# A recurrent-memory attention kernel: the forward loop's pools stay open, their tiles are reused by view in the backward loop, Wq is turned twice as often, and the crossbar loads are spread

## The chip, the core and the metric

The kernel runs on one core of one Trainium2 chip. Its time is the device time of one execution in microseconds (us); the time before is the median of three runs. One execution more was taken with the profiler. It gives for each instruction the engine, start, duration, and what it waited for. The engines are PE (matrix multiply; PEld are its weight loads), DVE (vector), ACT (scalar), POOL, and SP, which here only issues DMAs. ACT and POOL issue DMAs too.

## The reference

The reference is the forward pass and all gradients of a block with two branches. Branch B is a gated MLP. Branch A, which the change touches, is attention in 64 segments of 32 tokens, where eight memory rows pass from each segment to the next:

```
mem = mem0
for s in range(n_seg):                      # 64 segments
    h = concat([mem, xn[:, 32*s:32*s+32]])  # 8 + 32 rows, Dm = 640
    q, k, v = h @ Wq, h @ Wk, h @ Wv        # 32 heads of 128
    p = softmax(mask(q @ k.T * scale))
    o = (p @ v) @ Wo
    mem = o[:, :8]
    outs.append(o[:, 8:])
out = x + A(layernorm(x)) * silu(B(layernorm(x)))
grads = vjp(grad_out)                       # for x, mem0, Wq, Wk, Wv, Wo, w1, w3, w2
```

Only the eight memory rows are a chain from segment to segment, forward in the loop and backward in the gradient. The token rows can be computed at any time, and the kernel uses them to fill the gaps of the chain.

## The kernel before

The program runs in phases: layer norm and branch B forward, the first part of A, the forward recurrence (`recurrence`, L547), the backward recurrence (`phase4_Abwd`, L1073), then the weight gradients and B backward. The change lies in the two recurrences and between them.

**Forward recurrence.** `chain(t, gap)` (L591) does the memory rows of segment t; at named places (W0, W1, V0, W2, G1 to G6) it calls `gap`, which puts in token work of a block of three segments (`FILL`, L909). When the 64 steps are done, 13 units of token work (a block of 120 rows and four heads) are left. They are done in the tail (L1040), interleaved with a second stream, `work1` (L980), of which `fill(n)` takes n pieces. `work1` consists of:

- the first `out_proj` (L495), for the token rows 1344 to 1983. It takes 40 items: `ld` loads rows of 512 columns from the DRAM tensor OR (L509; a block that spans two stores takes two DMAs), `turn` transposes them on PE and copies them to oTm (L519, L520), `mm` multiplies by Wo (L526). Each item is two half items, with a yield after each. After eight items the sums are copied to `s_tok` (half on DVE, half on ACT) and stored to SR (L543). Six row buffers `orow` exist: four are quarters of the tile vt, two are tiles with the tag "kr" (L971, L972). Loads run five items ahead;
- beside every second half item, one turn of Wq (`wq_turn`, L717: five PE transposes of one head into bank bC and one copy to WqT, three in four on ACT, else on DVE);
- 16 gx blocks (`gx_block`, L1063: five matmuls of 512 columns, a copy, and after every second block a store to GX0);
- a second `out_proj` for the last 64 token rows, eight items.

The transposed weights WoT and WkT come through the crossbar: `turned_load` (L268), a transposing DMA issued by SP, 16 pieces each of 256x640 bf16 values. `w_ld(n)` (L712) issues n of those queued in `wfetch`. Of WoT, four go in gaps G2 and G4 of the last step and one in each step of the tail (L1050). WkT takes the place of Wq (tag "w2"), so it is allocated when Wq has been turned (L1002). Its pieces go with every second half item after that, with the gx blocks (L1014) and at the end (L1019).

**Backward recurrence.** `phase4_Abwd` opens pools of its own (L1094 to L1097) and makes its tiles (L1100 to L1110): four sets of row buffers (gors, gqvs, gPrs), and krb, which in the prologue serves as two more sets; vTb, which first holds gx blocks; gOTs, gdSs and others. Then come memsets on DVE (L1113), and banks in PSUM. The prologue (L1447 to L1474) does 19 units of token work: `ld`, `turn`, `dprob`, `dsoft`, `gmem`. It is interleaved with 32 further gx blocks (`gx_work`, L1432) and with 16 loads of WvT (L1464), which takes the place of Wo (tag "w3"). Then `chain` (L1171) goes from segment 63 to 0.

**What sets the order.** Each phase ends in `in_order(k, start)` (L273): it makes every instruction added since `start` follow the one written before it on its engine. An instruction written outside such a stretch, and two phases against each other, are ordered by the framework's scheduler, which takes what it finds ready; the wait for a buffer or a result is set by the framework too. When a pool is closed and another is opened over its addresses, the new pool's tiles wait for the readers and writers of the old pool as a whole. Inside one tile, reads and writes of different parts don't wait for each other.

Of the kernel before, what the change touches and what calls it, by code (L numbers as in the profile page):

```python
# [16 lines left out]
P = 128  # L17
# [371 lines left out]
def phase3_Afwd(k, W0, W4, Wv, Wk_):  # L389
# [4 lines left out]
    with tc.tile_pool(name="ast", bufs=1) as st:  # L394
# [5 lines left out]
        xPs = [st.tile([120, 4, P], BF16, name=f"xP{i}") for i in range(3)]  # L400
        PTs = [st.tile([120, 4, P], BF16, name=f"xPT{i}") for i in range(2)]
        oTm = st.tile([P, H, 32], BF16, name="oTm")
        first_part(k, Wv, Wk_, Wq, Wo, kTs, vt, hxs, qTs + xPs + PTs + [oTm])
        return recurrence(k, W0, W4, Wv, Wk_, Wq, Wo, kTs, vt, hxs, qTs, xPs, PTs, oTm)
# [90 lines left out]
def out_proj(k, Wo, x0, x1, acc, bank, orow, oTs, stok, q, done):  # L495
# [33 lines left out]
    for i in range(5):  # L529
        ld(i)  # L530
    yield
    turn(0)
    for i, (x, w, qd) in enumerate(items):
        ld(i + 5)
        turn(i + 1)
        mm(i, 0, 2)
        yield
        mm(i, 2, 4)
        if qd == 7:
            t = stok()  # L540
            for h in range(2):
                k.copy(t[0:w, 320 * h:320 * h + 320], acc[h][0:w, 0:320], eng='vs'[h])
            q.dma_start(k.SR[x:x + w, :], t[0:w, :])  # L543
        yield


def recurrence(k, W0, W4, Wv, Wk_, Wq, Wo, kTs, vt, hxs, qTs, xPs, PTs, oTm):  # L547
    nc, tc = k.nc, k.tc
    D, DC, S, H, HD, T = k.D, k.DC, k.S, k.H, k.HD, k.T
    with tc.tile_pool(name="achain", bufs=1) as ch, \  # L550
            tc.tile_pool(name="afill", bufs=1) as fl, \
            tc.tile_pool(name="aps", bufs=1, space=bass.MemoryType.PSUM) as ps, \
            tc.tile_pool(name="apm", bufs=1, space=bass.MemoryType.PSUM) as psm:
        bA, bB, bC = [psm.tile([P, 512], F32, name=f"bank{i}") for i in range(3)]
# [162 lines left out]
        def wq_turn(h):  # L717
            pt = bview(bC, P, DC, P, bf=True)
# [171 lines left out]
        def gap_of(t):  # L890
# [5 lines left out]
            def gap(g):  # L896
                FILL(g, t, at, kbatch)
                if t == T - 1:
                    if g == "G1":
                        w_alloc("o")  # L900
                        ld("q", *tail[0])
                        ld("q", *tail[1])
                    if g in ("G2", "G4"):
                        w_ld(2)
# [60 lines left out]
        batch = {t: b for t, b in batch.items() if t < T}  # L965
        for t in range(T):
            chain(t, gap_of(t))
        qm(T - 1)

        bA, bB, bC = [b_[:] for b_ in (bA, bB, bC)]  # L970
        orow = [vt[:, 512 * i:512 * i + 512] for i in range(4)]  # L971
        orow += [fl.tile([P, 512], BF16, name="orow", tag="kr", bufs=2)[:] for _ in range(2)]  # L972
        oTs = [oTm[:].rearrange("p a b -> p (a b)")[:, 512 * i:512 * i + 512].rearrange("p (a b) -> p a b", b=P) for i in range(2)]
        stok = lambda: ch.tile([P, D], BF16, name="s_tok", tag="oride")
        obank = lambda w: ps.tile([P, 4, w], BF16, name="opt", tag="x", bufs=5)
        done = {(k.NTL - 2, qd) for qd in SPL[0]}
        op = lambda x0, x1: out_proj(k, Wo, x0, x1, (bA, bB), obank, orow, oTs, stok, nc.gpsimd, done)
        X0, X1 = k.GB0, k.GB0 + 5 * P

        def work1():  # L980
            w_alloc("q")
            o = op(X0, X1)
            next(o)
            yield
# [7 lines left out]
            for _ in o:  # L992
                if n % 2 == 0 and n < 2 * H:
                    wq_turn(n // 2)
                n += 1
                yield
                if n == 40:
                    g_ld(0)
                if n == 2 * H:
                    while wfetch:  # L1000
                        w_ld(1)
                    w_alloc("k")  # L1002
                elif n > 2 * H and n % 2 == 0:
                    w_ld(1)
            g_ld(1)
            o = op(X1, S)
            next(o)
            for i, (x0, w) in enumerate(k.GXB[0:2]):
                for cg in range(4):
                    sg = ch.tile([P, 1024], BF16, name="g0st", tag="stg", bufs=2)  # L1010
                    for b in range(2):
                        gx_block(k, g0[i], sg, (bA, bB)[b], WT["o"], x0, w, cg, b, nc.scalar)
                        if b == 0:
                            w_ld(1)  # L1014
                        yield
            for _ in o:
                yield
            while wfetch:
                w_ld(1)  # L1019
# [4 lines left out]
        work = work1()  # L1024
# [15 lines left out]
        for i in range(len(tail) + 2):  # L1040
# [8 lines left out]
            if not WT.get("k"):  # L1049
                w_ld(1)  # L1050
# [22 lines left out]
def phase4_Abwd(k, out2, W4, WT):  # L1073
# [20 lines left out]
    with tc.tile_pool(name="gst", bufs=1) as st, tc.tile_pool(name="gchain", bufs=1) as ch, \  # L1094
            tc.tile_pool(name="gfill", bufs=1) as fl, \
            tc.tile_pool(name="gps", bufs=1, space=bass.MemoryType.PSUM) as ps, \
            tc.tile_pool(name="gpm", bufs=1, space=bass.MemoryType.PSUM) as psm:  # L1097
        NG = 4

        gors = [st.tile([120, 512], BF16, name=f"gor{i}") for i in range(NG)]  # L1100
        gqvs = [st.tile([120, 2, 512], BF16, name=f"gqv{i}") for i in range(NG)]
        vTb = st.tile([P, H, 40], BF16, name="vTt")
        bdm = st.tile([P, 16, 8], BF16, name="bdm")
        goxs = [st.tile([P, DC, 32], BF16, name=f"gox{i}") for i in range(2)]
        b16 = st.tile([P, 16], F32, name="b16")
        xpb = st.tile([P, 8, 2, 32], F32, name="xp")
        gdSs = [st.tile([120, 4, P], BF16, name=f"gdS{i}") for i in range(2)]
        gOTs = [st.tile([P, 4, P], BF16, name=f"gOT{i}") for i in range(2)]
        gPrs = [st.tile([120, 4, P], BF16, name=f"gPr{i}") for i in range(NG)]
        krb = st.tile([120, 2, 2048], BF16, name="krb")  # L1110
        bdf = goxs[0][:, 0:4, :].rearrange("p a b -> p (a b)").rearrange("p (a b) -> p a b", b=8)
        for tt in gOTs + gors + gdSs:
            nc.vector.memset(tt[:], 0.0)  # L1113
        bA, bB, bC = [psm.tile([P, 512], F32, name=f"gbank{i}") for i in range(3)]
# [19 lines left out]
        def loads(t):  # L1134
# [6 lines left out]
            Qst = ch.tile([P, 2, P], BF16, name="Qst", tag="Qst", bufs=2)  # L1141
# [4 lines left out]
        def load_k(t):  # L1146
            kr = krb[0:104, t % 2, :]
# [23 lines left out]
        def chain(t, gap):  # L1171
# [5 lines left out]
            bdP = ch.tile([P, 2, 16, 8], BF16, name="bdP", tag="bdP")  # L1177
# [54 lines left out]
            bdS = ch.tile([P, 2, 16, 8], BF16, name="bdS", tag="bdS")  # L1232
# [44 lines left out]
        def ld(tl, qd, eng=None):  # L1277
# [7 lines left out]
            if g < NG:  # L1285
                gor = gors[g][:]
                qv, Pr = gqvs[g][:], gPrs[g][:]
            else:
                x = xb[:, g - NG]
# [138 lines left out]
        xb = krb  # L1428
# [832 lines left out]
```

## Time and profile before

| | us |
|---|---|
| time, median of 3 runs (4725.97 to 4736.84) | 4726.07 |
| time of the profiled execution | 4735.54 |
| its span, from first to last instruction | 4733.5 |
| PE busy in the span | 4479.4 (95%) |
| DVE, ACT, POOL busy | 2245.7, 1587.4, 2096.0 |
| end of the last forward step's PE work | 1602 |
| last matmul of the first out_proj ends | about 1708 |
| last matmul of the second out_proj ends | 1748.6 |
| first gx matmul of the backward prologue | 1761.6 |
| first matmul of the backward chain | 1841.7 |
| end of the backward chain | about 2937 |

The lower rows are positions in the span, read from the lines of PE's work. A line of the timeline has start, duration, engine, line of the kernel, operation, output<-inputs and count; in square brackets is the idle time of that engine before it, and what ended it. A mean clock below 1.00 for PE in a stage says that the chip granted it less than full speed there. The DMA share is the mean busy share of the core's 16 DMA engines.

### The profile page before, as it was taken

How to read it: one execution, taken by the hardware profiler on the slowest of the kernel's cores; microseconds unless marked ns; L12 is line 12 of the kernel's file. 1: busy time of each engine (PE TensorE's matmuls, PEld its weight loads, DVE VectorE, ACT ScalarE, POOL GpSimd, SP SyncE). 2: the span in 40 equal slices, each digit the busy share in tenths (PEclk: the TensorE clock that was granted, in tenths of full speed). 3: DMA queues.
4: the chain of work that ended last, by engine and by line, in shares of the span. 5: the costliest groups of instructions: out<-in, count | busy, mean ns of one | idle time of the engine just before them, and what ended most of it. 6: DMA issues, size and time to landing. Idle time of an engine off the chain costs nothing. (4 is left out here: it accounts for less than half of the span.)

```text
span 4733.5 us, 160277 instructions
## 1 busy us (share of the span) xinstructions
PE 4479.4 (95%) x64504; PEld 2827.3 (60%) x64504; DVE 2245.7 (47%) x7155; ACT 1587.4 (34%) x4360; POOL 2096.0 (44%) x3520
## 2 busy tenths in 40 slices
PE   8998999999999887999999998999999999999999
PEld 4544555555555554666666665666666666666675
DVE  8734666666666534555555553332233322311460
ACT  5532555555544423333333332332223322200000
POOL 6522555555555413455444443553345533311340
PEclk9998999999999998999999998999999999999999
DMA  7773565666555578777777774754355543669683
GB/s 259 242 242 107 176 178 175 182 177 176 178 170 169 160 148 237 206 222 209 220 205 212 210 207 130 176 145 127 107 135 157 139 122 106 181 207 214 157 184 99
DMA packets 977448, 834.81 MB, mean 176 GB/s; under 512 B 518674, under 2 KB 859158, under 8 KB 974744
## 3 DMA queue, kind: packets, MB, share of 16 engines
q1 hardware_dynamic: 765871, 549.75, 42.1%
q0 software_dynamic: 129360, 227.19, 16.2%
q10 hardware_dynamic: 81475, 47.62, 3.9%
q8 instruction: 509, 8.34, 0.8%
q14 instruction: 233, 1.91, 0.2%
HBM read 472.66 MB, written 310.33 MB: 165 GB/s over the span
## 5 line engine op out<-in xcount | busy, mean ns | idle before, releaser
L1635 PE MATMUL wg<-gr,hr 128*128 128x512 bf16 x2400 | 521.7, 379 | 0.0
L1616 PE MATMUL g<-w,ghacc 128*128 128x320 bf16 x3072 | 460.4, 300 | 0.8
L1635 PEld LDWEIGHTS <-hr 128*128 128x128 bf16 x2400 | 234.1, 98 | 278.7
L1616 PEld LDWEIGHTS <-ghacc 128*128 128x128 bf16 x3072 | 288.7, 98 | 104.6 <-ACT ghacc L92 2.2
L306 PEld LDWEIGHTS <-hx 128*32 128x32 bf16 x7680 | 177.8, 97 | 174.4 <-issue 12.4
L90 DVE CAST wgo<-wg 128x512 bf16<-128x512 f32 x72 | 49.8, 692 | 471.2 <-PE wg L1635 471.2
L90 DVE CAST stg<-bank 128x512 bf16<-128x512 f32 x256 | 177.0, 692 | 168.4 <-PE bank L306 155.3
L873 POOL DMA_DIRECT2D OR<-xv x163 | 89.9, 552 | 369.7 <-ACT xv L92 345.6
L92 ACT COPY ghacc<-t6g 128x768 bf16<-128x768 bf16 (+1 forms) x176 | 137.1, 779 | 301.4 <-PE t6g L1598 298.8
L1581 POOL DMA_DIRECT2D GSP<-grs x48 | 25.7, 549 | 471.7 <-ACT grs L1573 471.2
L1312 POOL DMA_DIRECT2D VTD<-gvT x176 | 129.8, 745 | 236.3 <-ACT gvT L1311 201.3
L325 PEld LDWEIGHTS <-gkv 128*8 128x8 bf16 x8192 | 177.7, 86 | 80.5 <-DVE gkv L1184 3.5
L825 POOL TENSOR_TENSOR xP<-xP,xrz 120x480 bf16<-120x480 bf16 x163 | 161.3, 990 | 76.9 <-DVE xrz L824 48.2
L1622 DVE TENSOR_TENSOR ghacc<-ghacc,g 128x320 f32<-128x320 f32 x192 | 93.6, 487 | 210.2 <-PE g L1616 210.2
L805 ACT ACTIVATE xP<-xsp,xnm 120x120 bf16<-120x120 f32 (+1 forms) x540 | 186.1, 373 | 20.9 <-DVE xnm L787 18.4
L92 ACT CAST wgo<-wg 128x512 bf16<-128x512 f32 x48 | 28.1, 585 | 479.8 <-PE wg L1635 421.4
L1341 DVE SCALAR_TENSOR_TENSOR gdS<-gdp,Dx,gPr 120x120 bf16<-120x120 f32 (+1 forms) x680 | 182.9, 331 | 0.0
L1359 POOL DMA_DIRECT2D GXP<-gks x157 | 91.4, 582 | 189.7 <-ACT gks L1357 189.0
L325 PE MATMUL bank<-Wo,oTm 128*32 128x320 bf16 x4032 | 156.4, 310 | 18.6 <-DVE oTm L677 18.6
L306 PE MATMUL bank<-Wq,hx 128*32 128x512 bf16 x2560 | 163.7, 385 | 5.5 <-DVE stg L90 5.5
L325 PE MATMUL gbank<-WvT,gkv 128*8 128x320 bf16 x4096 | 167.0, 306 | 1.0 <-DVE gkv L1184 1.0
L245 POOL DMA_DIRECT2D r<-GOS x256 | 145.7, 573 | 42.9 <-issue 10.7
(365 smaller groups left out, 10935.6 us busy)
## 6 DMA issues: line engine op xcount, KB each, us to landing
QVS<-stg SPq DMA_DIRECT2D x128, 256.0 KB
gqv<-QVS SPq DMA_DIRECT2D x108, 192.0 KB
vTt<-VTD SPq DMA_DIRECT2D x64, 320.0 KB
PR<-xP POOLq DMA_DIRECT2D x168, 120.0 KB, 3.2
VTD<-gvT POOLq DMA_DIRECT2D x168, 120.0 KB, 3.9
DSR<-gdS POOLq DMA_DIRECT2D x168, 120.0 KB, 3.3
dS<-DSR SPq DMA_DIRECT2D x168, 120.0 KB
P<-PR SPq DMA_DIRECT2D x168, 120.0 KB
```

The source lines that it names most:

```text
L90: return nc.vector.tensor_copy(out, in_)
L92: return nc.scalar.copy(out, in_)
L245: eng.dma_start(d, src if src.shape[0] > 1 else src[0])
L306: k.nc.tensor.matmul(bank[32 * g:32 * g + 32, :], x[:, dc, :], W[:, dc, c0:c0 + 512], start=(dc == 0), stop=(dc == k.DC - 1), tile_positio ...
L325: k.nc.tensor.matmul(pm[p0:p0 + nq, 0:320], x[:, h, :], W[:, h, 320 * b:320 * b + 320], start=(first and i == 0), stop=(last and i == 15), ...
L805: nc.scalar.activation(Pb[0:n, j, 0:n], sp[0:n, j, :], ACT.Exp, bias=nmx[0:n, j:j + 1], scale=k.scale, accum_out=Z[0:n, j:j + 1])
L825: eng.tensor_tensor(Pb[0:n, :, 0:n], Pb[0:n, :, 0:n], bc_last(rz[0:n], n), ALU.mult)
L1312: nc.gpsimd.dma_start(k.VTD[tl][:, :, h0:h0 + 4, :], vTq[:])
L1341: nc.vector.scalar_tensor_tensor(dS[0:n, j, 0:n], dp[0:n, j, :], Dx[0:n, j:j + 1], Pr[0:n, j, 0:n], op0=ALU.subtract, op1=ALU.mult)
L1616: nc.tensor.matmul(pg[:], ring[:, i, j, r0:r0 + P], Ws[qd][i][:, j, 320 * h:320 * h + 320], start=(i == 0 and j == 0), stop=(i == 2 and j ...
L1622: nc.vector.tensor_tensor(a, a, pg[:], ALU.add)
L1635: nc.tensor.matmul(pw[:], hr[:, tl, dc * P:(dc + 1) * P], grs[i][:, tl, :], start=(tl == 0), stop=(tl == NF - 1))
```

## The change

It has these parts:

- `phase4_Abwd` is now called inside the forward part's pool "ast" and inside two PSUM pools that are opened once for both recurrences. Of its tiles, gors, gqvs, gPrs, vTb, gOTs, gdSs, Qst, bdP, bdS, gox and half of krb become views of kTs, vt, oTm, qTs, xPs, PTs and hxs. Only krb's other half, bdm, b16 and xpb stay new tiles. The pools "achain" and "afill" are still closed at the end of the forward part.
- `work1` is started earlier: its first piece, the loads of two rows of the first out_proj into the "kr" tiles, goes into gap G2 of the last forward step, ahead of the two crossbar pieces there. The other three loads of the run-ahead stay at the tail's start.
- Wq is turned with each of the first 32 half items, alternately into bank bC and into a slot of the five rotating PSUM slots "x".
- After the four crossbar pieces of the last step, one is issued with every third half item of the first out_proj, WkT's following WoT's, and those left go with every second pair of gx blocks and after them. The piece with each step of the tail is gone. The first gx load moves from half item 40 to 48.
- The SR stores are issued by ACT, not by POOL, and those of the second out_proj come out of a part of kTs[0], not of a tile of "achain".
- In the prologue three sets are loaded ahead of the two gx loads, not four; the memset that covered krb is one of two parts of it; the loads of WvT begin two steps earlier.

```diff
 def phase3_Afwd(k, W0, W4, Wv, Wk_, out2):
...
+        with tc.tile_pool(name="aps", bufs=1, space=bass.MemoryType.PSUM) as ps, \
+                tc.tile_pool(name="apm", bufs=1, space=bass.MemoryType.PSUM) as psm:
+            banks = [psm.tile([P, 512], F32, name=f"bank{i}") for i in range(3)]
+            own = kTs, vt, hxs, qTs, xPs, PTs, oTm
+            WT = recurrence(k, W0, W4, Wv, Wk_, Wq, Wo, own, ps, banks)
+            phase4_Abwd(k, out2, W4, WT, own, ps, banks)
...
 def out_proj(...):
-    for i in range(5):
+    for i in range(2):
+        ld(i)
+    yield
+    for i in range(2, 5):
         ld(i)
     yield
...
-            q.dma_start(k.SR[x:x + w, :], t[0:w, :])
+            nc.scalar.dma_start(k.SR[x:x + w, :], t[0:w, :])
...
         def wq_turn(h):
-            pt = bview(bC, P, DC, P, bf=True)
+            pt = bview(bC, P, DC, P, bf=True) if h % 2 else ps.tile([P, DC, P], BF16, name="wqpt", tag="x", bufs=5)[:]
...
+                    if g == "G2":
+                        next(work)
                     if g in ("G2", "G4"):
                         w_ld(2)
...
         def work1():
-            w_alloc("q")
+            orow.extend([fl.tile([P, 512], BF16, name="orow", tag="kr", bufs=2)[:] for _ in range(2)])
+            orow.extend([vt[:, 512 * i:512 * i + 512] for i in range(4)])
             o = op(X0, X1)
             next(o)
+            yield
+            next(o)
+            w_alloc("q")
             yield
...
             for _ in o:
-                if n % 2 == 0 and n < 2 * H:
-                    wq_turn(n // 2)
+                if n < H:
+                    wq_turn(n)
                 n += 1
                 yield
-                if n == 40:
+                if n == H:
+                    w_alloc("k")
+                if n == 48:
                     g_ld(0)
-                if n == 2 * H:
-                    while wfetch:
-                        w_ld(1)
-                    w_alloc("k")
-                elif n > 2 * H and n % 2 == 0:
+                if n % 3 == 0:
                     w_ld(1)
             g_ld(1)
-            o = op(X1, S)
+            o = op(X1, S, lambda: k0[:, 3072:3072 + D])
+            next(o)
             next(o)
...
-                        if b == 0:
+                        if b == 0 and cg % 2:
                             w_ld(1)
...
-            if not WT.get("k"):
-                w_ld(1)
...
 def phase4_Abwd(k, out2, W4, WT, own, ps, banks):
...
+        gors = [k0[0:120, 512 * i:512 * i + 512] for i in range(NG)]
+        gqvs = [two(ap[0:120, c:c + 1024]) for ap, c in ((k0, 2048), (k1, 1280), (k1, 2304), (om, 0))]
+        vTb = k1[:, 0:1280].rearrange("p (h c) -> p h c", c=40)
+        Qsts = [two(k0[:, c:c + 256]) for c in (3072, 3328)]
+        gPrs = [four(k1[0:120, 3328:3840])] + [x[0:120] for x in xPs]
+        gOTs = qTs[0:2]
+        gdSs = [qTs[2][0:120], PTs[0][0:120]]
+        bds = [PTs[1][:, 2 * i:2 * i + 2, :].rearrange("p a (h c) -> p a h c", c=8) for i in range(2)]
+        krbs = [st.tile([120, 2048], BF16, name="krb")[:], vt[0:120]]
...
+        for tt in gors + [t[:] for t in gOTs] + gdSs + [krbs[0][:, 1024:1536]]:
+            nc.vector.memset(tt, 0.0)
...
-        for _ in range(4):
+        for _ in range(3):
             ld_next()
         next(work)
-        nc.vector.memset(krb[:], 0.0)
         for _ in range(2):
             ld_next()
+        nc.vector.memset(krbs[1][:, 1024:1536], 0.0)
+        ld_next()
...
-            if 3 <= i < 19:
-                h0 = 2 * (i - 3)
+            if 1 <= i < 17:
+                h0 = 2 * (i - 1)
                 nc.sync.dma_start(WvT[:, h0:h0 + 2, :], k.WVT[:, h0:h0 + 2, :])
```

## The prediction, on record before the run

> **What bounds it now.** I read the page's forty slices first (PE is busy 80 to 99% of every slice, granted clock 0.9 or more), then the chain of waits, which covers only the last 6% of the span and doesn't reach the place of the change, then the busy time by stage. I cut the stages where the lines of PE's work change: the end of the forward chain, the fill with out_proj, the gx blocks, the second out_proj, the change of pools, the prologue of the backward loop (two pieces), the backward loop. The columns are the stage, its length, busy us and instructions of PE, PEld, DVE, ACT, POOL, then PE's clock, the DMA share and GB/s.
>
> ```profile
> 1602.00:1616.00 14.00, 2.94 (x32) 1.85 (x24) 4.22 (x12) 4.24 (x20) 6.38 (x9) 0.65 0.91 228
> 1616.00:1708.30 92.30, 84.22 (x917) 61.80 (x918) 38.45 (x118) 45.94 (x160) 23.55 (x45) 0.96 0.74 165
> 1708.30:1731.00 22.70, 17.91 (x83) 8.76 (x83) 5.52 (x9) 4.16 (x8) 0.55 (x1) 1.00 0.94 195
> 1731.00:1748.60 17.60, 13.62 (x96) 8.68 (x96) 2.35 (x9) 0.58 (x1) 0.00 (x0) 0.81 0.58 100
> 1748.60:1761.60 13.00, 0.42 (x8) 0.33 (x9) 4.31 (x10) 1.06 (x4) 4.45 (x8) 0.66 0.29 75
> 1761.60:1797.00 35.40, 33.29 (x298) 16.77 (x299) 16.56 (x107) 12.99 (x50) 12.44 (x22) 0.93 0.68 195
> 1797.00:1841.70 44.70, 28.16 (x311) 19.78 (x309) 25.06 (x140) 17.23 (x58) 18.72 (x33) 0.73 0.96 294
> 1841.70:2937.00 1095.30, 1040.64 (x24307) 679.87 (x24306) 561.87 (x2842) 349.77 (x1170) 510.67 (x926) 0.99 0.71 201
> ```
>
> The change acts on the 240 us from 1602 to 1842. There PE, the engine that sets the end everywhere else, stands still three times: 1602 to 1616, around 1708 to 1749, and almost wholly 1748.6 to 1761.6. From 1797 on DMA is the bound (share 0.96). The timeline of PE and of SP's queue says what ends the first two:
>
> ```profile
> 1613.99 0.59 PE L519 MATMUL opt<-ident,vt 128*128 128x128 bf16 x4 [5.78 <-DMA vt<-OR]
> ...
> 1716.73 4.48 PE L1067 MATMUL bank<-WoT,g0x 128*128 128x512 bf16 x20 [1.73 <-DVE g0st L90]
> ...
> 1740.84 0.37 PE L519 MATMUL opt<-ident,orow 64*128 64x64 bf16 x4 [3.70 <-DMA orow<-OR]
> ```
>
> ```profile
> 1720.18 14.83 SPq L270 DMA_TRANSPOSE WkT<-in_A_Wk_dram  x8
> 1735.06 1.07 SPq L509 DMA_DIRECT2D orow<-OR  x2
> ```
>
> At 1740.84 PE waits for rows that SP could issue only at 1735.06, because eight crossbar pieces stood before them for 14.83 us. At 1613.99 it is the same: the first rows of out_proj were issued behind four WoT pieces. The third standstill, in the timeline of all engines:
>
> ```profile
> 1749.52 0.54 POOL L543 DMA_DIRECT2D SR<-s_tok  x1 [40.11 <-ACT s_tok L92]
> 1751.96 0.64 SPq L265 DMA_DIRECT2D gqv<-QVS  x1
> 1751.97 0.66 DVE L1113 MEMSET gOT<- 128x256 uint32 x2 [3.00 <-DMA SR<-s_tok]
> ...
> 1758.83 2.55 SPq L270 DMA_TRANSPOSE vTt<-GS  x2
> ...
> 1761.60 5.81 PE L1067 MATMUL gbank<-WoT,vTt 128*128 128x512 bf16 x15 [6.07 <-DMA vTt<-GS]
> ```
>
> All of the backward part waits for the last store out of the forward part's pools (landed at about 1751.9), then loads, then computes: no overlap at all.
>
> **What the Trainium skill says.** "TensorE: Matmul & The Clock Gate", What's actually happening: after an idle window of some 3.4 us PE falls to half clock and needs about as long of work to return. The trace agrees: matmuls of 512 columns start 0.43 us apart at 1761.6 after the gap, 0.21 us later on. "DMA: Bandwidth & Descriptors", Anatomy of one DMA: about 2.0 us fixed cost, mostly completion; the last SR store here shows 2.0 us. The same page, Issuing engines are not separate DMA queues: moving a DMA to another engine saves only its issuing time; no row here contradicts it. The same page, Latency and other measured facts: 261 GB/s for a DMA transpose; here eight pieces of 256x640 bf16 (328 KB) take 14.83 us, 177 GB/s, so I use 1.85 us a piece packed, and 1.40 us of SP's time when spread (median of the WoT rows).
>
> **Part by part.**
>
> (a) Two of out_proj's row loads go into gap G2 of the last forward step, ahead of the WoT pieces. They are 4 DMAs of about 0.48 us, so the four pieces and the dump behind them on SP leave 1.9 us later. Item 0 and 1 then have their rows; the turn of item 0 needs only PE, free at about 1608 (its last work there ends at 1608.2). Item 2's rows come next on SP: 1610.5 + 1.9 = 1612.4, and 3.5 us until PE can use them (1610.47 to 1613.99 in the trace) gives 1615 to 1616, against 1620.57 for that turn now. **-5 us**, bounds -7 and -2.
>
> (b) Wq is turned every half item, not every second. PE's work is the same (32 x 0.28 us) and merely comes earlier. ACT gets 12 more copies of 692 ns in the first 40 us: 8.3 us on top of 21.4 busy from 1620 to 1660, so about 74%. Every second turn takes one of the five rotating PSUM slots that scores and transposes use. If each of these 16 waits out one copy, that is 11 us; freeing the second half of the loop from 16 turns can gain at most 4. Cover is ACT's idle quarter; I take **0**.
>
> (c) The crossbar pieces: before, 12 of WoT one per tail step and 16 of WkT packed from 1694.8 to 1735. After, one per three half items, so 26 of 28 in the loop of 80 half items. SP's queue in that loop now: 94 plain DMAs 48.3 us and 20 transposes 31.3 us, together 79.7 of 92.3 us. After: 27 transposes at 1.40 to 1.85 give 37.8 to 50, in all 86 to 98 us, and the loop would last some 87 without it. SP is then as full as PE, with five or six items loaded ahead as its only slack. The row loads, queued behind each piece, are what PE waits for. I charge **+3 us**, bounds 0 and +12. The loop then ends at 1708.3 - 5 + 3 = about 1706.
>
> What this buys comes after the loop, 1708.3 to 1748.6 (40.3 us). With no pieces in the way: 16 gx blocks of 5 matmuls at 0.215 us are 17.3 us; I leave 2 us for the two stages that still wait for their stores (three PE waits of 1.4 to 1.7 us now, DMA share 0.94). Eight items of the second out_proj take 1.4 us each at full clock (1731.60 to 1733.02, for instance), 11.2 us, for the 17.6 now with its 3.70 us wait and half-clock restart. 17.3 + 2 + 11.2 = 30.5, so **-10 us**, bounds -12 and -5.
>
> (d) Pools. The tiles of the backward prologue become views of kTs, vt, oTm and so on, whose last readers are done by about 1690 (kTs), and PSUM stays the same pool. So the loads, the memsets and the two vTt transposes need not wait for the end. Whether they leave early depends on order: each part writes its own order, but the memsets stand outside it and two parts may interleave. That it happens is seen at the other boundary:
>
> ```profile
> 2935.30 0.27 DVE L1509 MEMSET dST<- 120x256 uint32 x1 [3.22 <-PE gbank L325]
> ...
> 2937.79 0.55 DVE L336 TENSOR_TENSOR fsum<-gbank,fup 64x160 bf16<-64x160 f32 x2 [2.21 <-ACT fup L334]
> ```
>
> A memset of the next part runs on DVE before the backward loop's last sum. What remains in the new pools (gstg, gvT, krb) waits for the old achain and afill, whose last readers (orow in items 6 and 7) end 2.5 us before PE does; the SR store leaves from kTs and no longer counts. The fourth set of loads (a view of oTm) waits for the last matmul, but is used some 9 us later. So the 13.0 us become about 1 (the s_tok copies, 0.48, free the bank): **-12 us**, bound -5 if the memsets stay behind (then 0.5 us copies, 1.1 us memsets, three sets of loads, transpose and landing make about 7.5). The first 15 gx matmuls at full clock: 5.81 to 3.2, **-2**.
>
> (e) SR stores go from POOL to ACT's queue, 6 issues of about 0.3 us there; ACT would stand for DVE's half of the copy (1.3 us at 1639). ACT is half idle: 0, bound +6.
>
> (f) WvT's 16 loads start two units earlier, where the DMA share is 0.68 and not 0.96. Two loads of 328 KB at 294 GB/s leave the DMA-bound stretch: **-2**, bounds -3 and 0. That this stretch otherwise shifts as a whole, since its loads are released by its own buffers, is an assumption.
>
> (g) The backward loop, 64 steps of 17.1 us, keeps its instructions, and its views have as many copies as the tiles had: 0, bound in the rivals.
>
> Sum: -5 + 0 + 3 - 10 - 12 - 2 - 2 = **-28 us**. The profiled execution, 4735.5 us (4733.5 of span, 2 around it), would be 4707.5. It lies 9.5 above the median of three, 4726.07; the difference carries over: **4698 us**.
>
> **Rivals.** (1) SP becomes the bound of the loop: at 1.85 us a piece and plain DMAs stretched as in 1662 to 1708 (0.57 us each, where 0.51 is the mean), the loop ends 8 to 12 us later than I say; 4706 to 4710. For it: the sum in (c). Against: the pieces were slow when packed, not when spread. (2) The memsets and loads stay behind the forward part's last work: (d) gives -5 in place of -14, so 4707. Against: the 2935.30 line. (3) Slower: the views couple the backward loop. k0, k1 and oTm now hold buffers of different times, and if a load into one view waits for readers of its neighbour, SP, in order, holds everything behind it, vTt first, which the next step's PE needs. Its price is a part of a load's 2 to 3 us in each of 64 steps; 0.44 us a step eats the whole gain, 0.66 makes it slower by 0.3% (4740 us). Against: rows of vt are loaded now while neighbouring quarters are read, and SP's waits for those readers (L519) are 1.8 us in all from 1600 to 1750. (4) The change only moves waits: ACT and PSUM slots (b, upper bound 11) with (e) at 6 and (1) at its end: 4720 or so.
>
> **How the numbers follow.** Forecast 0.64, rival (1) 0.15, (2) 0.10, (3) 0.05, (4) 0.06. Better ends of the bounds (-7, -12, -3, no cost in c) reach 4688 to 4686; (1) and (2) reach up to 4710, and the range stops at 4713, with (3), (4) and a little else outside. About 0.3%, 14 us, is what can be told from no change: forecast, (2) and most of (1) are beyond it, 0.87; (4) and the rest within it, 0.08; slower, from (3), 0.05.
>
> **What would show it.** (a) The turn of item 2 at about 1615. (b) WqT copies ending at about 1655. (c) SP's queue without a run of pieces after the loop, the wait of 3.70 us on orow gone, DMA share in the loop near 0.9; wrong if PE shows repeated waits for DMA vt or orow in it. (d) First gx matmul of the backward part within 2 us of the last out_proj matmul, memsets and loads before it; wrong if SP's gqv loads follow that matmul. (g) Backward loop 1095 us, to within 5. The prediction is wrong if that loop changes by 20 us or if the first gx matmul comes after 1748.

## The result: 7 us faster, a quarter of the forecast

| | before | after | ratio, 95% interval |
|---|---|---|---|
| first measurement, median | 4732.32 us | 4724.47 us | 0.9985 (0.9978 to 0.9992) |
| a second one, later | 4731.64 us | 4724.38 us | 0.9984 (0.9976 to 0.9991) |

That is 7 us (4 to 11), where 28 were forecast. The profile of before that the prediction read turned out to be a long execution in places, so a second profile of each kernel stands beside it. Stages in us; "loop" is counted from the first matmul of the last forward step to the last one of the first out_proj, "chain" from the first matmul of the backward chain to that of its last step:

| stage | before, two profiles | after, two profiles | mean difference | forecast |
|---|---|---|---|---|
| loop | 119.0, 118.9 | 127.5, 126.5 | +8.0 | -2 |
| gx blocks and second out_proj | 40.7, 38.0 | 32.9, 34.7 | -5.6 | -10 |
| to the first gx matmul of the backward part | 13.0, 13.2 | 0.4, 0.4 | -12.7 | -12 |
| prologue | 80.1, 77.4 | 74.8, 77.0 | -2.9 | -4 |
| chain | 1080.3, 1081.7 | 1088.2, 1087.6 | +6.9 | 0 |
| sum | | | -6.3 | -28 |

The sum agrees with the measured 7 us. The rest of the program has the same instructions before and after; it differs by 5 us between the two profiles of before and by 7 between those of after, so a single stage is not certain to the microsecond.

The busy time by stage after (columns as before):

```profile
1581.30:1708.80 127.50, 103.78 (x1190) 71.22 (x1190) 52.52 (x158) 54.25 (x188) 34.40 (x62) 0.93 0.80 174
1708.80:1730.20 21.40, 18.11 (x84) 8.81 (x84) 5.88 (x9) 4.52 (x9) 0.00 (x0) 1.00 0.83 182
1730.20:1741.70 11.50, 11.23 (x100) 7.75 (x99) 2.77 (x11) 0.58 (x1) 0.00 (x0) 1.00 0.28 65
1741.70:1742.10 0.40, 0.26 (x8) 0.25 (x8) 0.35 (x1) 0.40 (x2) 0.14 (x1) 1.00 0.00 0
1742.10:1776.00 33.90, 33.50 (x321) 17.39 (x321) 17.27 (x108) 14.72 (x56) 15.99 (x29) 1.00 0.85 238
1776.00:1816.90 40.90, 25.62 (x297) 18.61 (x298) 24.44 (x138) 15.87 (x54) 17.37 (x29) 0.76 1.00 307
1816.90:2920.70 1103.80, 1047.13 (x24308) 681.53 (x24306) 561.48 (x2842) 350.61 (x1171) 509.64 (x926) 0.98 0.71 199
```

The second out_proj is full (11.23 of 11.50 us), the standstill between the parts is gone, and PE keeps its clock there. The loop has 1190 matmuls as before, in 8 us more. The same stages, from the gx blocks to the prologue, in the second profile of before:

```profile
1698.60:1721.90 23.30, 19.75 (x84) 9.44 (x84) 5.88 (x9) 4.52 (x8) 0.55 (x1) 0.93 0.89 186
1721.90:1736.60 14.70, 12.83 (x96) 8.36 (x95) 2.38 (x10) 0.58 (x1) 0.00 (x0) 0.88 0.52 122
1736.60:1749.80 13.20, 0.42 (x8) 0.46 (x10) 4.32 (x10) 1.06 (x4) 4.45 (x8) 0.63 0.31 80
1749.80:1784.00 34.20, 31.39 (x271) 15.86 (x276) 14.97 (x94) 12.06 (x46) 12.08 (x21) 0.90 0.66 194
1784.00:1827.20 43.20, 29.66 (x332) 20.97 (x332) 26.63 (x152) 18.62 (x61) 19.21 (x33) 0.78 0.96 303
```

The turn between the parts, after, in the timeline:

```profile
1727.90 2.56 SPq L270 DMA_TRANSPOSE kT<-GS  x2
...
1733.81 0.27 DVE L1126 MEMSET krb<- 120x256 uint32 x1 [1.23 <-DMA GX<-g0st]
...
1742.10 1.24 PE L1077 MATMUL bank<-WoT,kT 128*128 128x512 bf16 x5
```

Memsets and transposing loads run up to 14 us before the first gx matmul, which comes 0.4 us after the last one of out_proj, as forecast. In the loop, PE's wait for the third item and SP's queue ahead of it:

```profile
1600.76 1.06 PE L524 MATMUL opt<-ident,orow 128*128 128x128 bf16 x8
1610.04 0.59 PE L524 MATMUL opt<-ident,vt 128*128 128x128 bf16 x4 [4.79 <-DMA vt<-OR]
```

```profile
1595.47 1.82 SPq L514 DMA_DIRECT2D orow<-OR  x4
1597.33 3.41 SPq L270 DMA_TRANSPOSE WoT<-in_A_Wo_dram  x2
1600.84 0.52 SPq L612 DMA_DIRECT2D QVS<-stg  x1
1601.40 4.30 SPq L270 DMA_TRANSPOSE WoT<-in_A_Wo_dram  x2
1605.82 3.80 SPq L514 DMA_DIRECT2D vt<-OR  x8
```

Two items now start early, and the third waits 4.79 us behind the four pieces, as the first did before (5.78). Later the queue has next to no gap left:

```profile
1675.18 1.07 SPq L514 DMA_DIRECT2D vt<-OR  x2
1676.35 1.21 SPq L270 DMA_TRANSPOSE g0x<-GS  x1
1677.60 2.11 SPq L270 DMA_TRANSPOSE WkT<-in_A_Wk_dram  x1
1679.81 1.63 SPq L514 DMA_DIRECT2D vt<-OR  x2
1681.54 0.83 SPq L514 DMA_DIRECT2D orow<-OR  x2
```

```profile
1685.36 0.59 PE L524 MATMUL opt<-ident,vt 128*128 128x128 bf16 x4 [3.53 <-DMA vt<-OR]
```

The vt rows of 1679.81, meant to be loaded five items ahead, are the ones that PE stands for until 1685.36; then it runs at half clock. The buffer that they go into had been free since 1668.5, when PE's turn of the item six before ended. So SP came to this load 11 us after that, and the rows were used 5.6 us after it issued them: most of the delay arises in SP's queue. In all, SP's issues, summed from the timeline, fill about 91 of the 100 us from 1608.8 to 1708.8; before the change it was the prediction's 79.7 of 92.3.

### The profile page after: what moved, and what is told of

Same layout as the page of the kernel before. It is cut to its first block, busy times and chain, and to the rows that moved or that the text cites. A ratio compares the mean times of both kernels' runs of the same rounds, so it can differ in the third digit from the quotient of the medians.

```text
span 4720.1 us, 160254 instructions
## 1 busy us (share of the span) xinstructions
PE 4476.3 (95%) x64504; PEld 2824.1 (60%) x64504; DVE 2244.0 (48%) x7156; ACT 1588.8 (34%) x4360; POOL 2093.8 (44%) x3514
## 5 line engine op out<-in xcount | busy, mean ns | idle before, releaser
L306 PEld LDWEIGHTS <-hx 128*32 128x32 bf16 x10240 | 247.0, 96 | 233.8 <-issue 19.6
L336 DVE TENSOR_TENSOR fsum<-bank,fup 64x160 bf16<-64x160 f32 x254 | 69.5, 311 | 261.4 <-ACT fup L334 258.8
L325 PE MATMUL bank<-WvT,gkv 128*8 128x320 bf16 x4096 | 170.2, 310 | 0.0
L325 PE MATMUL bank<-WkT,gkv 128*8 128x320 bf16 x4096 | 162.8, 299 | 4.2 <-issue 2.5
```

The source lines that it names most:

```text
L306: k.nc.tensor.matmul(bank[32 * g:32 * g + 32, :], x[:, dc, :], W[:, dc, c0:c0 + 512], start=(dc == 0), stop=(dc == k.DC - 1), tile_positio ...
L325: k.nc.tensor.matmul(pm[p0:p0 + nq, 0:320], x[:, h, :], W[:, h, 320 * b:320 * b + 320], start=(first and i == 0), stop=(last and i == 15), ...
```

## The experiments

Times against the kernel before, measured beside each (ratio times its median); stages from one profile each.

| kernel | us (95%) | loop | gx, 2nd out_proj | turn | prologue | chain |
|---|---|---|---|---|---|---|
| after | -7.1 (-10.4, -3.8) | 127.5 | 32.9 | 0.4 | 74.8 | 1088.2 |
| pools_alone | -5.7 (-10.4, -0.5) | 119.3 | 40.2 | 0.4 | 74.6 | 1083.2 |
| tail_alone | +9.9 (6.6, 13.2) | 124.3 | 33.9 | 12.8 | 76.5 | 1085.1 |
| tail_again, the same | +11.8 (8.0, 16.1) | 127.4 | 34.1 | 12.5 | 78.1 | 1089.5 |
| rows_on_pool | -12.3 (-18.0, -6.6) | 124.8 | 31.7 | 0.4 | 75.7 | 1082.8 |
| spread_undone | -2.8 (-7.6, 1.9) | 119.9 | 42.4 | 0.4 | 74.6 | 1082.9 |
| turns_old | -11.3 (-17.0, -5.7) | 118.8 | 39.2 | 0.4 | 74.8 | 1083.6 |
| pieces_on_act | -0.5 (-4.7, 3.8) | 135.2 | 32.9 | 0.4 | 76.0 | 1081.8 |
| rows_joined | -10.9 (-14.7, -7.1) | 120.8 | 33.5 | 0.4 | 73.6 | 1087.8 |
| rows_first | -1.9 (-6.2, 1.9) | 131.3 | 32.2 | 0.4 | 75.0 | 1092.1 |
| joined_first | -6.2 (-10.4, -1.4) | 126.2 | 34.6 | 0.4 | 75.3 | 1087.6 |
| sr_on_pool | -10.4 (-14.7, -6.1) | 126.5 | 34.6 | 0.4 | 75.2 | 1079.9 |
| pools_pure | -15.6 (-19.9, -11.3) | 118.1 | 35.6 | 4.3 | 78.5 | 1075.1 |
| tail_pure | +3.8 (0.0, 7.6) | 126.6 | 32.4 | 13.2 | 77.1 | 1083.0 |
| joined_pool | -17.5 (-24.6, -10.9) | 120.6 | 33.2 | 0.4 | 76.4 | 1077.3 |
| joined_late | -20.3 (-27.9, -12.8) | 114.7 | 36.7 | 0.4 | 78.6 | 1075.1 |

**The two halves of the change.** First each half by itself, with the SR stores on ScalarE in both; and the two other ways of relieving SP.

> The kernel after with the last step's gap, the first projection loop, the rate of the Wq turns and the crossbar pieces put back as they were before; the pools kept open, the backward tiles as views, the SR stores on ScalarE and the earlier WvT loads stay. Theory Q (SP's queue, filled by the spread pieces, made the projection loop 8 us longer): the loop is back at 106 us, the part after it at 40, the turn from forward to backward stays at about 0.5 us instead of 13 and the prologue at 75 instead of 80, so 4 to 6 us off the kernel after and 12 to 18 off the kernel before. Theory V (the views couple backward steps through GpSimd, the 8 us that the backward loop grew): the backward loop is again near 1104 us, with matmuls waiting for the block-diagonal tile of GpSimd, and only some 10 us are off the kernel before. Theory S (the backward loop's 8 us are scatter between executions): 1096 to 1104 us, with long steps at other places than in the profile after.

> The kernel before with only the tail's part of the change: row loads of the first projection in the last step's gap, Wq turned twice as often, pieces spread one per three half items, SR stores on ScalarE; the pools are closed and opened as before. Theory Q: projection loop about 114 us, gx part and second projection about 33, the turn to the backward part 13 as before, so within 3 us of the kernel before. Theory V: backward loop 1096 us, since there are no views. Theory S: 1092 to 1104 us. If the loop's 8 us came of the scatter of one execution, the loop is at 104 to 106 here and the kernel is 8 to 10 us faster than before.

The loop belongs to the tail's half, as theory Q has it. Both halves came out worse than their stages: 5.7 us gained, where the stages of the profile sum to 13.5 less than the mean of before, and 9.9 lost, where they sum to 1.4 more. Much of that is scatter: the profiled executions, 4713.44 and 4728.02 us, lie 7.3 and 7.5 us under the medians of their kernels. Against V: tail_alone has no views, and its chain is no shorter (1085.1 us).

```
-            nc.sync.dma_start(orow[i % len(orow)][a:a + n, :], k.OR[...])
+            nc.gpsimd.dma_start(orow[i % len(orow)][a:a + n, :], k.OR[...])
```

> The kernel after with the row loads of both projections issued by GpSimd instead of SyncE, all else the same. Theory Q: SP keeps only the pieces and the q loads of the tail, the waits for vt and orow shrink from 10 us to under 3, the projection loop falls from 114 to about 104 us and the time by 8 to 10 us. Rival (the spread pieces cost the loop through the DMA engines or through ScalarE and the PSUM slots that the faster turns use, not through SP's order): the loop stays within 3 us of 114. A third way: GpSimd, which stands before xP and the v loads of the tail in its order, gets later and the waits for xP grow from 3 to 8 us or more, loop 112 to 118.

Inconclusive for Q, with the loop between the theories: without row loads between them, SP issued 11 pieces in one run of 23.04 us, the DMA share of the loop rose to 0.96, and the rows, landing 4 to 6 us after issue, were still waited for (11.2 us).

```
-                if n == H:
-                    w_alloc("k")
...
-                if n % 3 == 0:
-                    w_ld(1)
+                if n == 2 * H:
+                    while wfetch:
+                        w_ld(1)
+                    w_alloc("k")
+                elif n > 2 * H and n % 2 == 0:
+                    w_ld(1)
...
```

> The kernel after with the crossbar pieces at their places of before (one WoT piece a tail step, WkT from the 64th half item on, two half items apart, the rest packed after the loop); Wq is still turned twice as often and the row loads in the gap stay. Theory Q: the loop falls to about 105 us, the part after it goes back to about 40, the time is within 2 us of the kernel after. Rival (the doubled turns on ScalarE and in the PSUM slots made the loop longer): the loop stays at 112 to 114, the part after goes to 40, and the time is 6 to 8 us over the kernel after.

The loop is back at 119.9 us: its 8 us come of the spread pieces. What the spread bought after the loop (42.4 against 32.9) is about what it cost in it.

**Is the profile of before to be trusted, and is it SP?**

> The kernel before, unchanged, measured like the others: a second profiled execution of it, and its time against itself. If the profile of before shown so far was a usual execution, the stretch from the last forward step to the first backward step is again 253 us and the rest of the program again near 4481 us. The profiles of four changed kernels, each with its stages summed against that profile, promise 10 us more than their median times show; if that lies in the profile of before, its second profile is some 10 us shorter, and shows in which stage. The ratio should be within 0.1% of 1.

The ratio was 0.9999 (0.9990 to 1.0008). The stretch to the first backward step was 247.5 us, not 253: half of the riddle lay in that profile (prologue 80.1 against 77.4, second out_proj 17.6 against 14.7). The rest of the program was 4477.4.

```
                 if n % 3 == 0 and wfetch:
-                    w_ld(1)
+                    nc.scalar.dma_start_transpose(*wfetch.pop(0))
```

> The kernel after with the spread pieces of the projection loop issued by ScalarE in its own order instead of by SyncE; the four pieces in the last step's gaps and those after the loop stay on SyncE. Theory Q (SP's queue is the bound of the loop): the waits for vt and orow fall from 11 to some 6 us (those behind the four pieces stay), the loop from 127.5 us (counted from the last forward step) to about 121, 6 to 8 us off the kernel after. Theory E (the pieces take the DMA engines from the row loads, from whichever queue): waits for rows stay at 10 us or more, the loop at 125 or more. Where ScalarE stands for the 1.4 us of an issue, its exp and copies come later and the waits for xP and xv grow: a loop of 130 or more.

PE's waits in the loop, pieces on ScalarE:

```profile
PE bank L531 <- ACT s_tok L92: 5.2, 2, 3.0
...
PE opt L524 <- DMA vt<-OR: 3.0, 1, 3.0
...
PE opt L524 <- ACT xP L812: 2.5, 2, 2.0
```

and with them on SP, in the kernel after:

```profile
PE opt L524 <- DMA vt<-OR: 10.0, 5, 4.8
...
PE opt L524 <- DMA orow<-OR: 1.0, 2, 0.6
```

With the same pieces on another queue the waits for rows fall from 11.0 to 3.0 us. That points to SP's order rather than to the DMA engines. It isn't proof by itself, since the loop is also 7.6 us longer and gives the rows more time; the 11 us that the load at 1679.81 stood in SP's queue say the same. The price moves to ScalarE, whose queue is held 1.46 us by a piece (1644.86 in its timeline) and which is waited for instead: the loop of 130 us or more that the expectation named last came out at 135. This run is no version to keep: the Trainium skill, "DMA: Bandwidth & Descriptors", Latency and other measured facts, warns that two transposing DMAs in flight from different queues corrupt both outputs. No run here shows that.

```
...
+        dst, m = (orow[u], 1) if u < 2 else (pairs[u // 2 - 1], 2)
...
-            nc.sync.dma_start(orow[i % len(orow)][a:a + n, :], k.OR[..., 512 * qd:512 * qd + 512])
+            nc.sync.dma_start(dst[a:a + n, :], k.OR[..., 512 * qd:512 * qd + 512 * m])
```

> The kernel after with the rows of two neighbouring items loaded by one DMA of 1024 columns where their two buffers lie side by side (four items of six); the same bytes with a third fewer issues on SyncE. Theory Q: 27 of 80 half-microsecond issues go, 13 us of SP's time in the loop, so the loop falls from 127.5 to 119 to 122 us and the time by 6 to 8 us. Theory E (bytes on the DMA engines): at most 2 us.

As Q has it: the loop falls by 6.7 us to 120.8, with every piece still in it. The Trainium skill, "Perfetto Trace Analysis", What "DMA-bound" means, lists a solid track of the issuing sequencer as a bound of its own, against which large descriptors help. This run agrees: a row of a joined load is 1024 columns and not 512, and SP's issues fill about 78 of 94 us in place of 91 of 100. Joining also means fewer, larger pieces for the DMA engines, whose part in the gain this run doesn't separate; theory E, by bytes, allowed 2 us.

> The kernel with the pieces at their old places (the run before called spread undone), with Wq turned at its old rate as well; of the tail's change only the row loads in the last step's gap and the PSUM slots of the turns are left. In the run with the doubled turns the loop stood at 119.9 us, as with none of it (119.3), though it began 6 us sooner. Theory B (the doubled turns cost in ScalarE what the early rows give): the waits for xP and xv of ScalarE go and the loop falls to 114 to 116. Rival (the early start is given back in any case, at the item whose rows come behind the four pieces): 119 to 120 again.

The edit takes the kernel spread_undone and turns Wq at half items 0, 2, 4. Theory B fell: 118.8 us, against 119.9 with the doubled turns. The turns cost about 1 us in the loop. The medians of the two kernels lie further apart (11.3 and 2.8 us under the kernel before); the stages give 3.4 of these 8.5 us, and the rest is not explained, though the intervals just overlap. The early start is given back in any case, in the wait at the third item (4.98 us here).

**Mending the third item's wait.**

> The kernel after, unchanged, a second time: a second profiled execution, and its time on the chip of the two kernels that mend it. Expected: 0.9985 within 0.001; loop 125 to 128 us from the last forward step, the part after it 33, the backward loop between 1081 and 1088 (if the 1088 of its first profile was scatter) or 1088 again (if the views cost it).

Loop 126.5, chain 1087.6 again: scatter alone is an unlikely cause of the chain's 7 us.

> The kernel with the tail's part of the change alone, a second time. Its first measurement gave 10 us over the kernel before where its stages sum to no difference, and does not add up with the pools' part (5.5 us under) to the kernel after (7 under). If the parts add, 1.000 within 0.001 is expected here; if it is again 1.002, something outside the tail is slower in it, and its profile has to show where.

Again over 1.002, and the chain is 1089.5 us here, 8.5 over the mean of before. So there is a loss outside the tail, in kernels with and without views. That refutes V.

```
                     if g in ("G2", "G4"):
-                        w_ld(2)
...
             next(o)
             w_alloc("q")
+            w_ld(4)
             yield
```

> The kernel after with the four pieces of the last step's gaps put behind the first row loads of the projection (items 2 to 4) instead of ahead of them. Theory Q: the wait of 4.8 us for vt at the third item's turn goes (the tile is free from 1594.8 us on, SP comes to it at 1605.8), the half clock behind it shrinks, and the loop falls from 127.5 us by 4 to 6. Rival: the pieces, 8.4 us of SP, now stand ahead of the rows of items 5 and 6 and of the tail's q and v loads, and give the same wait there: the loop stays within 1.5 us.

The rival was right. PE's waits:

```profile
PE xpo L863 <- DMA xv<-QVS: 8.4, 1, 8.4
PE opt L524 <- DMA vt<-OR: 4.8, 4, 3.0
```

The four pieces, now packed (9.69 us on SP), stood before the tail's first v load. Here the wait was only passed on.

> Both mends at once: rows of two items by one DMA (loop 120.8 us) and the four pieces behind the first rows. Theory Q: the wait of 2.7 us left at the third item goes, loop 116 to 118, and the kernel 14 to 18 us under the kernel before. Rival: same as the joined rows alone, 12 us under.

The same wait of 8.4 us; 6.2 us under, worse than the joined rows alone.

**The chain's 7 us.** In the eleven profiles with the SR stores on ScalarE and nothing new on POOL, steps 13 and 19 of the chain take 18.3 to 21.0 us; in both of before, 17.0. Steps 7, 13 and 19 together are 8.6 and 4.9 us too long in the two profiles of after, about the whole of the chain's 6.9. POOL in step 13, first in the second profile of before, then after:

```profile
2056.41 0.55 POOL L1343 DMA_DIRECT2D DSR<-gdS  x1
2056.94 0.70 POOL L1479 DMA_DIRECT2D HRO<-FS  x1
2057.66 0.77 POOL L1169 TENSOR_TENSOR bdP<-bdm,gPm 128x128 bf16<-128x128 bf16 x2
```

```profile
2046.42 0.54 POOL L1355 DMA_DIRECT2D DSR<-xqT  x1
2048.66 0.70 POOL L1491 DMA_DIRECT2D HRO<-FS  x1 [1.70 <-DMA kT<-GX]
2049.38 0.77 POOL L1182 TENSOR_TENSOR xPT<-bdm,gPm 128x128 bf16<-128x128 bf16 x2
```

```profile
2049.84 0.62 PE L1195 MATMUL bank<-xPT,gOst 128*128 128x128 bf16 x2 [0.96 <-POOL xPT L1182]
```

POOL stands 1.70 us at a DMA, and the block-diagonal tile behind it (bdP, now a view of xPT) is late for PE. The releaser named is a guess; the second profile of after names none for the same stand. Counting POOL's DMAs from the start of the program, such stands come after numbers 949 (step 7), 1024 (step 13) and 1101 (step 19), the same in all eleven of these profiles. With the six stores on POOL, before the change and in the runs below, they come after 946, 1020, 1096 and 1174, before VTD stores of steps 6, 12, 18 and 24 that nobody in the step waits for. rows_on_pool, with 96 more DMAs on POOL, has steps 13 and 19 at 17.02 us too. Hence theory R and the last runs.

```
-            nc.scalar.dma_start(k.SR[x:x + w, :], t[0:w, :])
+            nc.gpsimd.dma_start(k.SR[x:x + w, :], t[0:w, :])
```

> The kernel after with one thing put back: the SR stores of both projections issued by GpSimd again instead of ScalarE (6 DMAs). Theory R (GpSimd's DMA issue stands for some 1.7 us once in about 75 of its DMAs; six DMAs fewer moved these stands in the backward loop from places where GpSimd has time to places ahead of the block-diagonal tile that the matmuls of a step wait for): the stands go back to the DMA numbers of the kernel before, steps 13 and 19 of the backward loop fall from 18.3 to 21 us to 17.03, the backward loop from 1088 to about 1082, and the time by 5 us or more against the kernel after. Rival (these steps are long for the spread or the views): they stay long. Cost of the stores on GpSimd in the loop: under 1 us.

```profile
2052.18 0.55 POOL L1355 DMA_DIRECT2D DSR<-xqT  x1
2052.71 0.70 POOL L1491 DMA_DIRECT2D HRO<-FS  x1
2053.43 0.77 POOL L1182 TENSOR_TENSOR xPT<-bdm,gPm 128x128 bf16<-128x128 bf16 x2
```

The stand is gone, steps 13 and 19 take 17.02 us, the chain 1079.9. Against the kernel before: 10.4 us, for 7.1 and 7.6; the intervals of these overlap, so by time this pair alone doesn't show the gain. The profiles do.

> The pools kept open and the WvT loads earlier, with all of the tail as before, the SR stores on GpSimd too: the pools' part of the change by itself. Theory R: backward loop 1081 to 1082 us, steps 13 and 19 at 17.03; the turn from forward to backward 0.4 us, prologue 75; so some 15 us under the kernel before, twice and more what the kernel with the stores on ScalarE showed (5.5 us). Rival (the views cost the backward loop): 1083 to 1088 and 5 to 7 us under.

15.6 us against 5.7 with the stores on ScalarE, intervals that don't overlap, and steps 13 and 19 at 17.02. The turn took 4.3 us here: the two transposes of GS stood behind row loads on SP (issued at 1737.02, not 14 us ahead), so its 0.4 us elsewhere hangs on the scheduler's order.

> The tail's part of the change alone (row loads in the gap, doubled turns, spread pieces) in the kernel before, with the SR stores left on GpSimd. With them on ScalarE it was 10 and 12 us over the kernel before in two measurements. Theory R says that about 5 of these belong to the stores: steps 7, 13 and 19 of the backward loop at 17 us, backward loop 1082 or less, and 3 to 7 us over the kernel before; with the pools' part alone (15.6 us under) that adds up to the kernel after with the stores on GpSimd (10.4 us under). Rival: again 10 us over, and the parts do not add.

3.8 against 9.9 and 11.8. Now the parts add: -15.6 + 3.8 = -11.8, measured -10.4. With the stores on ScalarE they could not, since their price was in both halves. The three pairs put that price at 3, 6 to 8, and 10 us.

**Versions without the faults.** joined_pool has both mends; joined_late also leaves out the gaps' four pieces, which fall after the loop:

```
             for _ in o:
+                w_ld(1)
                 yield
```

> The rows of two items by one DMA (loop 120.8 us, 12 us under the kernel before), and the SR stores back on GpSimd. Theory R: another 5 us in the backward loop, so 16 to 18 us under the kernel before. Rival: 12 us under, with steps 13 and 19 long.

> As the run before (joined rows, SR stores on GpSimd), and the four pieces of the last step's gaps left to the spread, so that four more fall after the loop, one per half item of the second projection, where SP stands idle for 10 us. Theory Q: the wait of 2.7 us for the third item's rows goes, and the loop falls from 121 to 117 or 118; the part after it stays within 2 us of 33; so 18 to 20 us under the kernel before. Rival (the pieces cost 1.9 us each wherever they lie): no gain on the run before, the loop shorter and the part after it longer by the same.

17.5 and 20.3 us, the best of the series, as Q and R gave: joined_late has a loop of 114.7 and a chain of 1075.1. The part after the loop took 36.7, where 31 to 35 was expected: the pieces aren't free there either. Step 13 is 17.02 in both, but step 19 takes 18.3 with no stand of POOL in it, which was not traced. The two versions cannot be told apart by their intervals, nor from pools_pure (11.3 to 19.9 us), which leaves the tail as it was; that a mended tail gains anything is not shown by time.

## Why the prediction was wrong

The tail's part failed: (a), (b) and (c) came to -12, and tail_pure measured +3.8 (0.0 to 7.6). The third error is (e), which put the moved stores at nothing. The pools' part, (d) and (f), came to -16, and pools_pure measured -15.6. That close a match is partly luck: by its profile 8.8 us came from the turn and next to nothing from the prologue, and the rest from the chain and the stage of the gx blocks, where these terms forecast no gain. Step by step, from the stages:

(a) "-5 us", the early rows: **0**. Item 2's turn came 28.7 us after the last step's start (31.7 and 31.4 before), so 3 us earlier and not 5; and these don't reach the loop's end. In turns_old, which has the early rows, PE's waits in the loop add up to 16.1 us, against 19.0 in the second profile of before, but its matmuls are busy for 102.4 us, not 99.9: PE runs twice at half clock, at item 0 (granted clock 0.51 from 1602.7 to 1605.7) and, after the wait, at item 2 (0.77 from 1612.7 to 1619.7), where in before it did so once, after its wait. I had moved a wait and counted it as shortened.

(b) "0": right in the loop, about 1 us (turns_old).

(c) "+3 us" in the loop, bounds 0 to 12: with what it promised after the loop this is the largest error. The sum was there, SP 86 to 98 us full in a loop of 87; I took 3 of the up to 11 us that the sum lay over the loop, because spread pieces are short. Measured: SP taken for about 91 us, spread_undone against after 7.6 us, rows_joined 6.7 back. The loop ends 10 us later than forecast, as rival (1) had it, but 5 of these are (a). PE's seven waits for rows sum to 11.0 us. The two long ones, 4.79 and 3.53 us, were followed by half clock; the five shorter ones, up to 0.8 us, were not. After the loop "-10 us" was -5.6: the second out_proj is as computed (11.5 for 11.2), the gx blocks took 21.4 and 23.0 us for 19.3, still waiting for their stores, and the 40.3 us of before were 38.0 in the second profile.

(d) "-12 us": right, -12.7, in every kernel with the views but pools_pure, where the order kept 4.3 us; rival (2) had named that dependence. The clock's and WvT's share, -4, was -2.9.

(e) "ACT is half idle: 0, bound +6": the reason held for ACT (the loop is 126.5 us with the stores on POOL, 127.5 and 126.5 on ACT); I had counted only the issuing time that moves, and had not asked what the stores' leaving does on POOL's queue. **+7 us** by the chain's length (3 to 10 by whole times), some 300 us later, in a loop whose instructions are the same. This alone is a quarter of the forecast.

(g) "0", and rival (3), the views: right on the views. pools_pure, with all of them, has a chain of 1075.1 us.

In sum the miss of 22 us is 10 in the loop (5 each from a and c), 7 from the moved stores, 4 after the loop (c), 1 in the prologue.

Two sums of the forecast were off: its better ends (-7, -12, -3, no cost in c) give 4690, not 4688 to 4686, and rival (4), with 11, 6 and the upper end of (1), gives about 4727, not 4720. Neither changes the forecast.

Open: why POOL stands at its DMAs and what exactly is counted, how much of the rows' lateness the DMA engines add, and why the prologue differs by up to 5 us between profiles of like kernels. The scatter of the untouched stages was not traced to a cause.

## What to carry to other kernels

Before work is spread into a stage, add up the issuing queue's time there, and if it reaches the stage's length, price the overflow in full and ask which load stands behind each piece; fewer, larger DMAs shortened the loop here (120.8 us), where another order did not (131.3). A DMA moved to another queue changes the sequence on both, so look for stands of the queue it leaves in every loop downstream. Take two profiles before reading a stage's length to the microsecond, and see how far each profiled execution lies from its kernel's median before setting stages against times.

## What the runs showed of the hardware

POOL stood 1.7 to 1.8 us at one of its DMAs about every 75 (after numbers 949, 1024, 1101). The stand doesn't keep its place in the program: with six stores more on POOL it came 9 to 11 DMAs earlier there. Nor is the plain number of DMAs fixed, since by that count it came after 946, 1020 and 1096. It goes with what the queue issued before, in a measure that was not found; no wait in the trace explains it.

PE's clock after step 13's wait, in the kernel after:

```profile
2044.21:2049.80 5.59, 4.62 (x90) 3.09 (x91) 3.05 (x16) 3.21 (x11) 3.23 (x7) 1.00 0.67 210
2049.80:2053.30 3.50, 3.33 (x52) 1.91 (x55) 0.42 (x1) 0.37 (x1) 2.42 (x4) 0.52 0.82 235
2053.30:2056.80 3.50, 3.50 (x49) 1.53 (x42) 1.47 (x7) 0.00 (x0) 0.00 (x0) 0.51 0.80 238
```

A wait of 0.96 us was followed by 7 us at half clock, and the step took 20.95 us in place of 17.02. The second profile of after has the same wait in the same step, and there the clock stayed full and the step took 18.34 us:

```profile
2061.36:2064.86 3.50, 3.33 (x84) 2.24 (x87) 1.29 (x5) 0.36 (x1) 2.41 (x4) 1.00 0.74 208
2064.86:2068.36 3.50, 3.50 (x104) 2.34 (x100) 3.16 (x21) 1.09 (x4) 0.00 (x0) 1.00 0.93 291
```

Of the eleven profiles with this wait, the clock fell below full in seven. The Trainium skill, "TensorE: Matmul & The Clock Gate", What's actually happening, speaks of an idle window of some 3.4 us; here a wait of 1 us was enough in some executions and not in others, and the measurement decides. What makes the difference is not shown.
